# A new table of order, engines and PSUM banks for a fused attention and gated feed-forward kernel on one core

## The chip, the cores and the metric

The kernel runs on one core of a Trainium2 chip. The metric is the device time in microseconds (us) of one execution, the median of several runs. A core has five engines with a queue of instructions each: PE (TensorE, matmuls and transposes), DVE (VectorE), ACT (ScalarE), POOL (GpSimd) and SP (SyncE, which only issues transfers here).

## The reference

Eight batches, twelve heads, 448 positions, 64 elements a head. Attention's result, laid out as 448 x 768 for each batch, is the input of a gated feed-forward part with a convolution of three taps along the positions:

```python
q_n = q / sqrt(mean(q * q) + 1e-6) * g_q          # the same for k
attn = softmax(q_n @ k_n.T / 8)                   # (8, 12, 448, 448)
x = (attn @ v).transpose(0, 2, 1, 3).reshape(8, 448, 768)
h = maximum(x @ w_in, 0)                          # w_in 768 x 1024, float64
conv = sum(conv_w[k] * h shifted by k - 1 for k in range(3))   # along the 448 positions
out = (h * sigmoid(conv)) @ w_out                 # w_out 1024 x 768, float64
```

## The kernel before

Heads are worked in pairs, n = 0 to 47, six pairs to a batch. For each pair: squares of q and k (`square`), their sums and reciprocal roots (`square_sum`, `rsqrt`), q and k divided by them (`apply_rms`, 112 x 512 tiles named sq), transposes of these on PE (L812, tile sq to a bank, then copied as kT and qT), scores (L993) in groups of two tiles of 128 query rows and 448 keys, a row maximum (`soft_max`, DVE, L999, tile sst), an exponential (`soft_exp`, ACT, L1007, tile e), the transpose of e, and the product with v (pv, L1120). Pairs 0 to 9 are worked in float32: e is transposed on PE (`p_transpose`, L1038) and copied from the bank to PT (`p_evac`). From pair 10 on, operands are split into a float16 high part and a float16 low part: e into ph (`p_hi`, L438, and `p_lo`, L450), which a transfer transposes, and v into vp (`v_hi`, L442 or L444, and `v_lo`, L1105 on DVE, or two instructions on POOL). Before that a maximum of v is taken (`v_bound`, L899 or DVE's L901). A group's scores are written to two PSUM banks, and each bank is free again when the exponential of its tile has read it.

The results of six pairs make x for one batch (`x_hi`, `x_lo`). Its feed-forward part multiplies x with w_in (L1201), applies relu, the three taps and the gate, splits the result (`in_hi`, `in_lo`, tile gring), and multiplies with w_out (L1270), then copies the result out of PSUM (`out_evac`) and stores it.

w_in and w_out come as float64. Each is loaded in parts (blocks), which DVE converts to float32 by three integer instructions a part (L577, L581, L585); a bound of its absolute values is taken (L636, ACT), a power of two as scale is made from it, and each block of 128 rows is then split: `split` writes the float16 high part of a block of w_in (128 x 1024) or w_out (128 x 768), and `rest` the low part (L673 on DVE; L670 and L671, two instructions, on POOL). The trace shows these tiles as wi or wo, since they share buffers.

All of this is a list of 4,976 steps. The order is written out by hand: in the table ORDER a step has a place of two digits to the base 85, in ENGINES a letter (T PE, V DVE, A ACT, G POOL, S SP), and in BANKS the numbers of the PSUM banks that it writes. The loop at the end sorts the steps by their place and issues them, so that each engine's queue is the sorted list cut down to that engine. An engine works its queue in this order; a library puts in the waits for data and for buffers. There are 8 banks and few buffers: four e, four ph, two sq, two vp, eight v.

The lines that a choice of engine touches:

```python
def copy_scaled(e, dst, src, scale):
    if e == "ACT":
        nc.scalar.activation(dst, src, AF.Copy, scale=scale)
    else:
        elementwise(e).tensor_scalar(dst, src, scale, None, op0=ALU.mult)
...
def split(_, c):
    z = w32[:, c + 1, :]
    copy_scaled(on["split", name, c], dst[:, 0, c], z, sc)
```

Of the kernel before, what the change touches and what calls it, by code (L numbers as in the profile page):

```python
# [41 lines left out]
    bound_row="4L9X",
    bound_spread="4Q9i",
    scale="4S9l",
    in_factor="7N",
# [19 lines left out]
    rsqrt=(
        "090C0F0H0L0P0R0U0W0M0Q0S0V0X0c0f0h0k0d0m0o0s0y0&0*0<110x0z0(0+0=0_101A1E1s1u1y1#1%1;1=1^"
        "222{2|3033363D3F3I3f4t4v4x4(4-4=4@5B5F6(6+6<6?6{6}737M7R8g8k8o8s8x8$8+8=90A#A+A;A~B1BFBP"
        "BVBhDCDLDUDXDpDtDyD!D&FiFqFsF&F)F<F@F^F}H-H@H`H}I4ILITIdIhKtKuKwK&K_K~L1L7LDM;M=M?M_M|N1"
        "N2NENHP6PAPDPFPUPWPdPgPlRkRoRxR(R-R=R?R_S7T@T_T|U0U4U5U9UAUHWRWVWYWkWlWqWuW%W*Y=Y?Y_Y}Y~"
        "Z0Z2Z5Z7bNbPbSbfbhbibmbobsdXdadddmdzd%d?d_d`g8gCgFgKgLgOgQgUgYiSiViYiaibifigijipk!k#k&k*"  # L70
        "k=k@k_l7l9nZnandngnknlnnnqnvptpvpzp#p;p@p`q3q7"
    ),
# [21 lines left out]
    scores=(
        "0%0>121V1b1x1+2g2l2(373R3s3y4W4b4p525I5T5#5|6A6V6q6&787%7;8W8d8}9L9$ASAVB9BDB-B>CkCpCsDW"
        "DaE2E7EtExFHFLFOF$GtGvG_H|I2ItIxJZJdJ~K2KvKyLGLILLL?MXMZNNNQNUOCOFPTPYQ9QEQeQ!Q(RnRrR^R}"
        "S$S(S+ThTjU6USV6VBVwV#W)W=XTXmXsYNYQZ4Z8ZcZfZ_Z|a+a;bJbdbkcaccdxd$eTeXe$f1f5f&g3g6g!h6hB"
        "hHh-h?iWirjYjbkGkJlClFljl&mSmXm<m>m`nyn#o8oDo`pFpIqDqHq*q<r<r?sIsnsrtMtO"
    ),
    soft_max=(  # L100
        "0@0`16181B1K1d1q1z1)1-23262O2n2q2y2_31393K3T3m3w3z3$3)3;4c4f4r4$4}505J5L5U5X5j5n5-5?6669"
        "6N6T6j6s6%6-6@727P7U7=7?7`858f8u8#8>95979a9q9;A6AWAZAgA-BHBKBOBxB?C3C8CECrCvC&C{DEDIDbDe"
        "D(D-EAECENETE!E*E-E`FNFPFTFgFnF!F>GiGyG$G>G^G~HBI6I9IHIMI!I>I|J8JeJhJlJoK4K8KAKFK!K)K>K|"
        "LKLOLQLULjL_M4M7MaMdM*N4NRNTNXNbNkNxOJOROgOzPZPiPzP^QGQIQNQWQlQ$Q;Q^R7RDRtRwR#R&R~SHSOSU"
        "S*S;S^T0TMTQTkTnT&T?UEUOUkUoVCVHVPVTV&V_V}WBW>W^X5XDXXXeX#X(X*X~YRYTYfY$ZAZDZPZRZgZoZxZ@"
        "a6aDaUada<a^a{b0bWbZblbuc8cKcecicqc>d)d{e3eLeYecegeke;e`fBfJfNfhf=f^g7gGgkgpg)g+hGhIhRhV"
        "hYhwh{i4i6iAieiviyi{jcjgjlj?kMkXkek$lGlJlOlklyl@l{m5mZmdmumyn0n3n6nCnDnrn$n+n}oEoHoKoWoo"
        "p1pDpKpOpapcqMqPqeqlr0rBrKrMr@r`r~s4sNshsss$s_s{tPtRtXti"
    ),
# [1295 lines left out]
```

## Time and profile before

| | |
|---|---|
| median of 3 runs | 806.04 us (804.91 to 807.04) |
| time of the profiled execution | 805.12 us |
| its span in the profile | 803.3 us |
| PE busy | 780.5 us (97%) |
| DVE, ACT, POOL busy | 712.0, 637.5, 450.7 us |

The span runs from the first to the last instruction that the profiler saw, and the time of the execution is 1.82 us longer. A busy share is the part of the span in which an engine had an instruction under way. PEclk is the clock that TensorE was granted, 1.00 being 2.4 GHz and 0.50 being 1.2 GHz. Arrows in a row of the trace name the engine and tile that ended an engine's idle time.

### The profile page before, as it was taken

The page shows a single profiled execution, that of the slowest core. Times are in us where ns is not written, and L with a number is a line of the kernel's source. Part 1 is how long each engine was busy: PE and PEld are TensorE (multiplying, and loading weights), DVE is VectorE, ACT ScalarE, POOL GpSimd, SP SyncE. Part 2 cuts the span into 40 slices and gives each one's busy share as a digit, 9 for nine tenths or more (in the row PEclk, how much of TensorE's full clock was granted, in tenths as well). Part 3 has the DMA queues.
Part 4 walks back from the last instruction along what each step waited for, and adds up shares of the span by engine and source line. Part 5 has one row for each costly group of instructions (what it writes and reads, how often), then busy time and mean ns, then how long its engine had stood idle before and what let it go on. Part 6 is the DMA issues. An engine that isn't in the chain of part 4 may idle for free.

```text
span 803.3 us, 16861 instructions
## 1 busy us (share of the span) xinstructions
PE 780.5 (97%) x5564; PEld 421.6 (52%) x5564; DVE 712.0 (89%) x1489; ACT 637.5 (79%) x1542; POOL 450.7 (56%) x552
## 2 busy tenths in 40 slices
PE   3998999999999999999999999999999999999998
PEld 1545555555554555555555555555555555555554
DVE  7999999999999889998899988999999899992560
ACT  5999999997898777998788868998799767862221
POOL 2556246766478457766696646885487543530020
PEclk9999999999999999999999999999999999999999
DMA  8864653499998989999899999999999998846002
GB/s 246 236 193 116 172 179 101 97 186 208 187 199 183 195 177 209 194 182 195 188 188 199 200 181 199 207 190 197 191 189 180 209 196 182 160 91 150 12 1 79
DMA packets 345704, 137.46 MB, mean 171 GB/s; under 512 B 285376, under 2 KB 342032, under 8 KB 345616
## 3 DMA queue, kind: packets, MB, share of 16 engines
q1 hardware_dynamic: 345616, 136.37, 79.9%
q8 instruction: 44, 0.72, 0.4%
q14 instruction: 44, 0.36, 0.1%
HBM read 56.65 MB, written 11.18 MB: 84 GB/s over the span
## 4 chain that ended last, share of the span: by engine, by line
PE 55%; DVE 1%; ACT 1%; issue 1%; POOL 0%; ACTq 0%
PE bank L1270 21%; PE bank L1201 17%; PE bank L1120 7%; PE bank L993 7%; PE bank L1038 1%; PE bank L812 1%; ACT e L1007 0%; PE bank L1068 0%; DVE c L1221 0%; DVE ph L450 0%; POOL ph L450 0%; ACT PT L438 0%; ACT ph L438 0%; ACT sq L741 0%; ACT bank L1209 0%
## 5 line engine op out<-in xcount | busy, mean ns | idle before, releaser
L1201 PE MATMUL bank<-x,wi 128*128 128x448 f16 x1152 | 236.6, 353 | 0.8 <-DVE c L1231 0.6
L450 POOL TENSOR_TENSOR ph<-e,ph 128x448 f16<-128x448 f32 x139 | 148.8, 1073 | 93.9 <-ACT ph L438 60.9
L1270 PE MATMUL bank<-wo,gring 128*128 128x384 f16 (+1 forms) x1056 | 191.7, 327 | 0.0
L1201 PEld LDWEIGHTS <-wi 128*128 128x128 f16 x1152 | 110.1, 98 | 102.0 <-issue 12.8
L1270 PEld LDWEIGHTS <-gring 128*128 128x128 f16 (+1 forms) x1056 | 100.4, 99 | 65.1 <-issue 10.8
L993 PE MATMUL bank<-kT,qT 64*128 64x448 f16 (+3 forms) x1072 | 128.1, 390 | 3.8 <-ACT e L1007 2.2
L1120 PE MATMUL bank<-PT,vp 112*64 112x448 f16 x912 | 93.1, 354 | 0.0
L450 POOL TENSOR_TENSOR sq<-qkf,st 112x512 f32<-112x512 f32 x73 | 80.1, 1108 | 17.9 <-DVE st L773 7.2
L1221 DVE SCALAR_TENSOR_TENSOR c<-bank,cwb,c 128x447 f32<-128x447 f32 x128 | 85.8, 675 | 3.1 <-ACT c L442 2.1
L438 ACT CAST ph<-e 128x448 f16<-128x448 f32 x141 | 78.4, 561 | 2.1 <-DMA PT<-ph 2.0
L1120 PEld LDWEIGHTS <-vp 112*64 112x64 f16 x912 | 48.9, 110 | 41.0 <-issue 11.2
L1038 PE MATMUL bank<-ident,e 128*112 128x128 f32 x432 | 64.1, 281 | 0.0
L752 DVE TENSOR_REDUCE st<-sq 112x16 f32<-112x1024 f32 (+1 forms) x50 | 58.1, 1167 | 4.2 <-ACT sq L741 4.1
L450 DVE TENSOR_TENSOR ph<-e,ph 128x448 f16<-128x448 f32 x89 | 58.1, 655 | 2.8 <-POOL ph L450 1.2
L1038 PEld LDWEIGHTS bank<-ident,e 128*112 128x112 f32 x432 | 49.7, 136 | 20.0 <-ACT e L1007 5.6
L993 PEld LDWEIGHTS <-qT 64*128 64x128 f16 (+1 forms) x912 | 33.7, 97 | 49.4 <-issue 28.9
L442 ACT ACTIVATE c<-bank,vsc 128x384 f32<-128x384 f32 x45 | 25.8, 580 | 41.1 <-PE bank L1270 41.0
L450 POOL TENSOR_TENSOR gring<-c,gring 128x448 f16<-128x448 f32 x32 | 34.8, 1088 | 38.2 <-ACT gring L438 36.4
L741 ACT ACTIVATE sq<-qkf 112x1024 f32<-112x1024 f32 (+1 forms) x47 | 47.9, 1021 | 6.5 <-DMA qkf<-in_q_dram 4.3
L1227 ACT ACTIVATE c<-c 128x448 f32<-128x448 f32 x64 | 36.5, 573 | 17.3 <-DVE c L1221 13.7
L450 POOL TENSOR_TENSOR x<-x,x 128x448 f16<-128x448 f32 x34 | 37.9, 1116 | 21.7 <-DVE x L438 15.2
L450 POOL TENSOR_TENSOR qkf<-sq,qkf 112x512 f16<-112x512 f32 x35 | 42.5, 1213 | 9.9 <-DVE qkf L438 6.1
(1148 smaller groups left out, 1588.0 us busy)
## 6 DMA issues: line engine op xcount, KB each, us to landing
qkf<-in_k_dram SPq DMA_DIRECT2D x48, 224.0 KB
v<-in_v_dram SPq DMA_DIRECT2D x48, 224.0 KB
rB<-rd SPq DMA_DIRECT2D x96, 112.0 KB
out_dram<-c SPq DMA_DIRECT2D x56, 192.0 KB
wo<-in_moe_w_in_dram SPq DMA_DIRECT2D x12, 512.0 KB
gring<-in_moe_w_out_dram SPq DMA_DIRECT2D x16, 384.0 KB
qkf<-in_q_dram SPq DMA_DIRECT2D x24, 224.0 KB
qkf<-in_q_dram SPq DMA_DIRECT2D x48, 112.0 KB
```

The costliest lines, as they stand in the source:

```text
L438: (nc.scalar.copy if e == "ACT" else elementwise(e).tensor_copy)(dst, src)
L442: nc.scalar.activation(dst, src, AF.Copy, scale=scale)
L450: elementwise(e).tensor_tensor(dst, a, b, op=op)
L741: nc.scalar.activation(sq, x, AF.Square)
L752: nc.vector.tensor_reduce(st, sq, axis=AX.X, op=ALU.add)
L993: nc.tensor.matmul(ps[u][o, :S], lhs, rhs, start=(i == 0), stop=(whole(m) or i == 2),)
L1038: nc.tensor.transpose(ps[:PB, kt * P : (kt + 1) * P], e[:, kt * PB : (kt + 1) * PB], ident)
L1120: nc.tensor.matmul(ps[HALF[h], :S], lhs, rhs, start=(i == 0 and k == 0), stop=(i == pvs(n)[-1] and k == NB - 1),)
L1201: nc.tensor.matmul(ps[:, :S], wi[:, wl, c, fc * P : (fc + 1) * P], old("x", b * NP + c)[:, xl], start=(i == 0), stop=(i == 3 * NP - 1),)
L1221: nc.vector.scalar_tensor_tensor(c[:, dst], h[:, src], w[:, tap, fc : fc + 1], c[:, dst], op0=ALU.mult, op1=ALU.add)
L1227: nc.scalar.activation(c, c, AF.Tanh)
L1270: nc.tensor.matmul(ps[p0 : p0 + m, :NO2], g, wo[:, wl, fc, half * NO2 : (half + 1) * NO2], start=(i == 0), stop=(i == 3 * NFC - 1),)
```

## The change

The code stays as it is; the numbers in ORDER, ENGINES and BANKS are others. Of the table ORDER two lines show the form:

```diff
-    split="4Z4o4*4~5p5(9p9y9<A5AKAsA<B8",
+    split="4Y4q4+4|5l6M9p9z9=A2ALAzA~BM",
```

The letters that give a step to another engine, for four of the names:

```diff
-    split="A",
+    split="AAAAAGAAAAAAAG",
-    square="AAAAAAGAAGAAAGAAAAAAAAAAAAAAAAAAAAAAAAAAAAAAAAAAAA",
+    square="AAAAAAGAAGGAAGAAAAAAAAAAAAAAAAAAAAAAAAAAAAAAAAAAAA",
-    v_hi="AAAAAAVAAAAAAAAAVVVAAAAAAAAAAAAAAAVAAV",
-    v_lo="V",
+    v_hi="AAGGAAAAAAVGGVAAAAAGGVAAAAAGAAVAAAGGAV",
+    v_lo="VVVVVVVVVVVVVVVVVVVVVGVVVVVVVVVVVGGGGV",
```

So POOL (G) gets the split of block 5 of w_in and of the last block of w_out, the square of pair 8, nine of the 38 `v_hi` and five of the 38 `v_lo`. Counted over all names, before and after: `p_evac` 103 on ACT and 5 on DVE, then 97 and 11; `p_hi` 45 on POOL, 141 on ACT and 42 on DVE, then 60, 134 and 34; `p_lo` 139 on POOL and 89 on DVE, then 137 and 91; `x_lo` 34 on POOL and 14 on DVE, then 38 and 10; `in_hi` 18 on POOL, 38 on ACT and 8 on DVE, then 16, 35 and 13; `in_lo` 38 on POOL and 26 on DVE, then 35 and 29; `out_evac` 45 on ACT and 11 on DVE, then 40 and 16. `convert` stays on DVE and the bounds of the weights on ACT. PE has the same steps in both, and so has SP, in slightly other orders.

Three places are shown in the order of one engine.

PE, where pair 4's scores begin; e0 and e1 are tiles of pair 3 that are transposed, sq_5 is pair 5's normalized q and k, kT_4 and qT_4 the operands of pair 4's scores. A group of scores writes two banks. Before:

```order
L1038 MATMUL bank2_68<-ident_83,e0_74 112x128 x4
L1038 MATMUL bank3_69<-ident_83,e1_75 112x128 x4
L558 LDWEIGHTS ones_85
L558 MATMUL bank7_73<-mrow_84,ones_85 128x1
L812 MATMUL bank6_72<-ident_83,sq_5_513 128x112 x4
L993 MATMUL bank4_70<-kT_4_686,qT_4_710 128x448
L993 MATMUL bank1_67<-kT_4_686,qT_4_710 128x448
L993 MATMUL bank2_68<-kT_4_686,qT_4_710 128x448
L993 MATMUL bank5_71<-kT_4_686,qT_4_710 128x448
L993 MATMUL bank4_70<-kT_4_686,qT_4_710 128x448
L993 MATMUL bank3_69<-kT_4_686,qT_4_710 128x448
```

The same place now:

```order
L812 MATMUL bank3_69<-ident_83,sq_5_510 128x112 x4
L558 LDWEIGHTS ones_85
L558 MATMUL bank7_73<-mrow_84,ones_85 128x1
L993 MATMUL bank1_67<-kT_4_703,qT_4_676 128x448
L993 MATMUL bank4_70<-kT_4_703,qT_4_676 128x448
L1038 MATMUL bank7_73<-ident_83,e0_74 112x128 x4
L1038 MATMUL bank6_72<-ident_83,e1_75 112x128 x4
L993 MATMUL bank2_68<-kT_4_703,qT_4_676 128x448
L993 MATMUL bank5_71<-kT_4_703,qT_4_676 128x448
L993 MATMUL bank4_70<-kT_4_703,qT_4_676 128x448
L993 MATMUL bank3_69<-kT_4_703,qT_4_676 128x448
```

Two transposes of pair 3 now stand between the first group of scores and the second, and the third group's first bank, bank 4, is held by the first group's second tile and no longer by its first.

ACT, the same place; PT_3 is a copy of a transposed tile of pair 3, e0 and e1 from sst_(4_0 and sst_(4_1 are the exponentials of pair 4's first two tiles, wi32 with wsc a split of w_in. Before:

```order
L1007 ACTIVATE e3_77,rsum_3_611<-bank4_70,sst_(3_6_667 128x448
L438 COPY PT_3_642<-bank2_68 112x4x128
L442 ACTIVATE wi32_92<-wi32_92,wsc_96 128x1024
L442 ACTIVATE kT_5_764<-bank6_72,G_82 128x448
L438 CAST x_1_770<-x32_1_671 128x448
L438 COPY PT_3_642<-bank3_69 112x4x128
L1007 ACTIVATE e0_74,rsum_4_776<-bank4_70,sst_(4_0_761 128x448
L442 ACTIVATE wi32_92<-wi32_92,wsc_96 128x1024
L1007 ACTIVATE e1_75,rsum_4_776<-bank1_67,sst_(4_1_766 128x448
```

And now:

```order
L1007 ACTIVATE e3_77,rsum_3_597<-bank4_70,sst_(3_6_668 128x448
L442 ACTIVATE kT_5_738<-bank3_69,G_82 128x448
L438 COPY PT_3_640<-bank2_68 112x4x128
L442 ACTIVATE wi32_92<-wi32_92,wsc_96 128x1024
L438 COPY PT_3_640<-bank5_71 112x4x128
L1007 ACTIVATE e0_74,rsum_4_771<-bank1_67,sst_(4_0_762 128x448
L1007 ACTIVATE e1_75,rsum_4_771<-bank4_70,sst_(4_1_765 128x448
L438 COPY PT_3_640<-bank7_73 112x4x128
L442 ACTIVATE wi32_92<-wi32_92,wsc_96 128x1024
L438 COPY PT_3_640<-bank6_72 112x4x128
```

The two exponentials now follow each other, the cast of x_1 has left ACT, and two copies of PT stand behind the exponentials.

POOL, about pairs 6 to 8; sq_6 and sq_7 with st are `apply_rms`, x_3 and x_4 high and low parts of x, rsum the denominators. Before:

```order
L450 TENSOR_TENSOR sq_6_722<-qkf_6_525,st_6_721 112x2x4x64
L438 CAST x_3_980<-x32_3_963 128x448
L1062 TENSOR_SCALAR rsum_5_892<-rsum_5_892 128x7
L450 TENSOR_TENSOR sq_7_753<-qkf_7_665,st_6_721 112x2x4x64
L450 TENSOR_TENSOR x_3_980<-x32_3_963,x_3_980 128x448
L438 CAST x_4_1105<-x32_4_1093 128x448
```

And now, where the row with 112x1024 is the square of pair 8 and the row with 128x1024 the split of block 5:

```order
L450 TENSOR_TENSOR sq_6_723<-qkf_6_636,st_6_722 112x2x4x64
L450 TENSOR_TENSOR sq_8_985<-qkf_8_709 112x1024
L450 TENSOR_TENSOR sq_7_746<-qkf_7_670,st_6_722 112x2x4x64
L438 CAST x_3_1016<-x32_3_979 128x448
L450 TENSOR_TENSOR x_3_1016<-x32_3_979,x_3_1016 128x448
L444 TENSOR_SCALAR wi32_92<-wi32_92,wsc_96 128x1024
L1062 TENSOR_SCALAR rsum_5_891<-rsum_5_891 128x7
L438 CAST x_4_1114<-x32_4_1095 128x448
```

Both new rows stood on ACT before.

## Rows read from the trace of the kernel before

**Rows 1.** The page's busy time, share of the span and instructions of each engine

```profile
PE 780.5 (97%) x5564; PEld 421.6 (52%) x5564; DVE 712.0 (89%) x1489; ACT 637.5 (79%) x1542; POOL 450.7 (56%) x552
```

**Rows 2.** Windows: stretch, length, busy PE, PEld, DVE, ACT, POOL, PEclk, DMA share, GB/s

```profile
0.00:10.60 10.60, 0.01 (x1) 0.01 (x1) 6.02 (x28) 3.99 (x7) 2.79 (x11) 1.00 0.71 212
10.60:62.38 51.78, 46.75 (x271) 25.51 (x271) 50.77 (x128) 47.83 (x124) 24.15 (x34) 1.00 0.80 219
62.38:66.00 3.62, 1.77 (x8) 0.69 (x9) 3.52 (x5) 3.62 (x8) 2.98 (x2) 1.00 0.81 260
66.00:71.00 5.00, 5.00 (x26) 3.93 (x26) 4.98 (x10) 4.51 (x9) 3.80 (x9) 0.66 0.47 113
71.00:101.61 30.61, 30.29 (x192) 15.78 (x191) 30.23 (x61) 30.22 (x75) 11.83 (x18) 1.00 0.55 149
101.61:780.00 678.39, 676.97 (x4931) 365.19 (x4930) 615.24 (x1261) 543.84 (x1317) 403.39 (x478) 1.00 0.84 171
780.00:803.30 23.30, 19.68 (x143) 10.54 (x140) 1.24 (x2) 3.49 (x6) 1.72 (x2) 1.00 0.19 68
```

**Rows 3.** PE's waits, whole span: bank and line, releaser, us, times, longest

```profile
PE bank L812 <- POOL sq L450: 11.1, 2, 10.6
PE bank L993 <- ACT e L1007: 2.2, 2, 1.8
```

**Rows 4.** PE's longest wait between 101 and 780 us, same columns

```profile
PE bank L1201 <- DVE c L1231: 0.6, 1, 0.6
```

**Rows 5.** PE in time: start, length, instruction, [idle before, releaser]

```profile
62.38 1.77 PE L993 MATMUL bank<-kT,qT 64*128 64x448 f32 x8
66.00 1.02 PE L993 MATMUL bank<-kT,qT 64*128 64x448 f32 x4 [1.84 <-ACT e L1007]
66.95 4.08 PE L1038 MATMUL bank<-ident,e 128*112 128x128 f32 x20
...
85.03 0.60 PE L812 MATMUL bank<-ident,sq 112*128 112x112 f32 x4
...
98.77 1.96 PE L1038 MATMUL bank<-ident,e 128*112 128x128 f32 x16
...
101.61 1.31 PE L1201 MATMUL bank<-x,wi 128*128 128x448 f16 x6
```

**Rows 6.** One window of 1 us, columns as in rows 2

```profile
67.00:68.00 1.00, 1.00 (x7) 0.99 (x6) 1.00 (x3) 0.60 (x2) 0.60 (x2) 0.50 1.05 222
```

**Rows 7.** ACT in time: the exponential of pair 4's first tile

```profile
65.19 0.67 ACT L1007 ACTIVATE e<-bank,sst_(4_0_761 128x448 f32<-128x448 f32 x1
```

**Rows 8.** ACT's groups: shapes, count, busy us, mean ns, idle before

```profile
L438 ACT COPY PT<-bank 112x512 f32<-112x512 f32 x68 | 38.3, 598 | 0.9 <-PE bank L1038 0.5
L438 ACT CAST x<-x 128x448 f16<-128x448 f32 x24 | 13.5, 563 | 1.9 <-DVE x L1131 1.9
L899 ACT ACTIVATE vabs<-v 112x512 bf16<-112x512 f32 x29 | 18.3, 631 | 1.0 <-DVE vacc L896 0.7
L442 ACT ACTIVATE wi<-wi,wsc 128x1024 f16<-128x1024 f32 x6 | 7.1, 1182 | 0.0
L741 ACT ACTIVATE sq<-qkf 112x1024 f32<-112x1024 f32 x43 | 45.4, 1058 | 0.7 <-issue 0.7
```

**Rows 9.** Groups of POOL, and one of DVE, same columns

```profile
L670 POOL TENSOR_SCALAR wo<-wo,wsc 128x768 f32<-128x768 f32 x1 | 2.2, 2212 | 0.0
L438 POOL CAST qkf<-sq 112x512 f16<-112x512 f32 x10 | 6.7, 672 | 0.3
L450 POOL TENSOR_TENSOR ph<-e,ph 128x448 f16<-128x448 f32 x139 | 148.8, 1073 | 93.9 <-ACT ph L438 60.9 <-DVE ph L438 18.0 <-issue 3.4
L450 DVE TENSOR_TENSOR ph<-e,ph 128x448 f16<-128x448 f32 x89 | 58.1, 655 | 2.8 <-POOL ph L450 1.2 <-ACT ph L438 0.9 <-issue 0.4
```

**Rows 10.** POOL and DVE in time: a square on POOL, the rest of block 5

```profile
62.50 1.89 POOL L450 TENSOR_TENSOR sq<-qkf 112x1024 f32<-112x1024 f32 x1 [7.48 <-PE bank L812]
...
92.39 1.28 DVE L673 SCALAR_TENSOR_TENSOR wi<-wi,wsc 128x1024 f16<-128x1024 f32 x1
```

More of the change, by code (lines that the diff above doesn't have):

```diff
@@ L30 @@
     load_g="05",
-    make_g="0Y",
-    load_cw="3=6e4j",
+    make_g="0X",
+    load_cw="3H6S5|",
     make_cw="8(",
-    load="02080K0N0u0;0|1e1k2I2j2-2>3O4T4Y5D5Q5)626a6p7G7O7(868Z8v",
+    load="02080J0N0g0;1H1X1h1?2j2+2<3h4S4d5B5W5;5^6j6r7G7Y7-868b8y",
     convert=(
-        "0A0D0G0g0i0t0!0)0-0}131S1P1Z1f1v1$1}1?2V2f2a2i2)2c2$42353a452}3P3^3h3r3|4C4F4O4A4D4I4<53"
-        "5851555E5r5x5$5v5_5}6L6Q6W6f6i6l6|767B797E7J7p7w7!7*7}828K8O8T8j8l8q8`91999B9D9J"
-    ),
-    bound="0J0$0?2~2M2B2@2^4E4B44497q6X6d7T7L7k7<8h7)7n8a8e98969F9O",
@@ L40 @@
-    bound_max="4H9R",
+        "0A0D0G0h0j0v0$0*0<111A1T1R1W1e1v1$1+212V2d2R2i2(2m2$43393W3|2{3O413f3p3@4C4F4N4A4D4I4;52"
+        "57545A5J5r5z5&5w5$5+6W6d6h6f6i6o75787C7E7K7N7r7y7&7=7~828N8P8W8k8p8t8_8}949B9D9G"
+    ),
+    bound="0q0%0@2^202F312;4E4B48457D6e5}7s7d6)7(8D7?7b8l8U969C989L",
+    bound_max="4H9Q",
     bound_turn="4J9U",
[L42 to L45, printed above, removed]
-    split="4Z4o4*4~5p5(9p9y9<A5AKAsA<B8",
-    rest="4i4w4^5a5y6Y9u9&9`ABARA$B2Bq",
@@ L48 @@
-    out_factor="A!",
+    bound_row="4L9Y",
+    bound_spread="4O9d",
+    scale="4R9g",
+    in_factor="7H",
+    split="4Y4q4+4|5l6M9p9z9=A2ALAzA~BM",
+    rest="4j4x4@5Z5t6Y9u9*9`AAAUA+B5Bv",
+    out_factor="A%",
     load_k=(
-        "00040T0q1M2F2<3-4a5s6J7j7~9+AzCMDRElFuG-IKJXKnMCNIOGPvQ#R@T4UmVjWWY5Z$anbrcoe!fSgwh!j>j~"
-        "mRmwo|p3"
+        "00040S0s1k2L3u3=465p6J7l8B9$AsCNDPE(G6G%ILJaKpM6M(OJPiQ;ScTKU{VRWhY2ZaaicPckd{fNgqhzjVj~"
+        "lkmzo<o`"
     ),
     load_q=(
-        "030B0a0#1t2R3j464d5+6=7m8^9>A&CQD_EyG6G`I#JjK*MGN`OUP@Q&SgTIU?VlX8YBZ(aqcScre%fVg|h&j_k3"
-        "mqm!p0p7"
+        "030B0b0w1p2P3y3}4g626P7u8)9)AwCRD=E@GSG-J4JeLYM9NrONPnQ?SnTWVIVfWnY7ZjaocVcoeefRgzh%j=k3"
+        "mhm&o@o}"
@@ L64 @@
+        "ktkzn9nOpYph"
     ),
     rsqrt=(
[L66 to L70, printed above, removed]
@@ L93 @@
+        "oKoZoboc"
     ),
     scores=(
[L95 to L98, printed above, removed]
+        "0&0>131U1c1y1(2g2l2&383S3s3x4Q4k4p505H5X5<5`666Z6$6*797$7;8c8f8|9K9-ASAYB8BDB-B>CoCrCwDN"
@@ L103 @@
[L103 to L107, printed above, removed]
@@ new lines @@
+        "s`t*uZug"
+    ),
+    v_max="2O7hDSL|RCaBg!oi",
+    v_turn="2T7pDuMASQaHg)ol",
+    v_row="2a7vEKMCSqaJg>oo",
+    v_spread="2f7!ETMISuaXh4or",
+    v_scale="2r7*EWMKSwabh8ox",
+    qk_lo="9oAxClDDE`F7GwH;K1KvL*MNO6O*Q&RaTXUHVCWFXfYyZ)atcJdue#fog}hrjEkKmZm;oAo>q&rp",
+    q_hi="9V9XByCiD}FCGJGyIvJ_LJL+NlNjP;QlSfT3UoVKXBYSZnaGbzccesflh9h3j0j$l^m*oSoHqYrQ",
+    q_lo="9a9kB*CnE3FFGOG+I!J~LsM3NsOWP@Q^SkTHUtVvXKYaZ$ajb)cneyf$hDh?j6j|l|n2oYokqdrV",
+    q_turn="9lAZB_CxEOFNGYH&I;KBL!MTN!O!QARTSrT$U#V}XcYoa6b0b^d6e*f<hLiDjjk_mQn7ogpaqqsF",
@@ L266 @@
+        "tcuRuxu8wVwQwHwawFwSwgwj"
     ),
```

336 lines of the change are left out of this document (168 added, 168 removed).

## The prediction

> **What bounds the kernel now.** The page's busy times come first: PE is busy for 780.5 of 803.3 us [rows 1], so whatever the table does elsewhere can only reach the time through PE, and PE has the same 5,564 matmuls before and after. Three things of PE can move: its idle time, its clock, and what it loses between instructions of different kinds. The windows say where these lie [rows 2]; in each the reader should compare the length with PE's busy time. The span has 22.8 us without a matmul: 10.6 at the start, 5.0 up to 62.38, 1.85 from there to 66, 0.3 from 71 to 101.61, 1.4 in the 678 us up to 780, and 3.6 at the end. The list of PE's waits names them: one wait of 10.6 us for the first normalized tile, and one of 1.8 us in which scores wait for an exponential [rows 3]. After 101 us the longest is 0.6 us [rows 4].
>
> The wait of 1.84 us is the one to look at closely. In PE's timeline [rows 5] two groups of pair 4's scores run at 62.38, and the third starts at 66.00, released by ACT. Directly behind it the granted clock falls: it is 0.50, the 1.2 GHz level, in the window from 67 to 68 [rows 6] and 0.66 on average from 66 to 71, against 1.00 in every other stretch [rows 2]. Twenty transposes then take 4.08 us where sixteen take 1.96 at the full clock [rows 5]. The fall costs 5.0 x 0.34 = 1.7 us; the transposes alone give 4.08 - 1.96 x 20 / 16 = 1.6, which agrees. So this place costs 3.5 us, a third of the 10 us that PE loses between its start and its tail.
>
> Last come the other engines' shares in the same windows. From 62.38 to 101.61 ACT is busy for 38.4 of 39.2 us and DVE for 38.7; from 101.61 on ACT has 135 us to spare, DVE 63 and POOL 275 [rows 2]. So until about 101 us PE's progress is set by ACT and DVE, whose exponentials free the score banks; later it is set by PE itself.
>
> **The start.** Up to the first scores the rows of DVE, POOL and SP are the same in the order of both, and ACT and DVE have the same steps ahead of the exponentials of pairs 0 and 1. Nothing is taken for it, neither gain nor loss.
>
> **The wait at 66 us.** Before, the third group's first bank is held by pair 4's first tile, whose exponential starts at 65.19 and takes 0.67 [rows 7], so it ends just when PE starts. Now the bank is held by the second tile. Ahead of that exponential ACT loses two copies of PT and the cast of x_1: 2 x 0.598 + 0.563 = 1.76 us by the means of their groups. It gains the second exponential, 0.67 by the first's row, and the bound of v for pair 6, 0.63 [rows 7, 8]. Net, the release comes 0.46 earlier; instructions on ACT overlap by about 0.1 us, so I take **0.3 us**. From both sides: nothing, if the two copies were hidden behind other waits, and 1.0 if the bound is hidden.
>
> What becomes of the idle time is less plain. The two transposes of pair 3 that ran ahead of the scores now stand between the first and second group, and the second group's banks come free by copies that stand behind a split on ACT (1.18 us [rows 8]). So the one wait is cut into two or three, some of it ahead of the first group, with 1.1 us of transposes and 0.9 of scores in between. I expect no single stretch as long as 1.84 us, and the only such stretch in the trace that is followed by a lower clock after the start is that one. My forecast is that the fall goes: **-1.7 us**, with 0 as the other end, if a stretch of that length merely moves forward.
>
> **What the lead can be worth.** -0.3 and -1.7 would be -2.0 at 71 us, but it has to survive to 101.61, through a stretch in which ACT is full. Ahead of the last exponentials there ACT loses two casts of x (0.56 each), the split of block 5 (1.18), the square of pair 8 (1.06) and a copy of PT (0.60), together 3.96; it gains a bound of v (0.63), a copy of PT (0.60), and two short steps that I bound by 0.6 each, together 2.4 [rows 8]. The difference, -1.5, is how much sooner ACT can be through. ACT's idle time from 66 to 101.61, 0.49 + 0.39 [rows 2], could be squeezed out as well, which makes 2.4 the upper end. DVE gives up three of the steps that ACT gains and one more, some 1.8 us or more at ACT's prices, so ACT is the limit. I take the lesser of 2.0 and 1.5: **-1.5 us** in all up to 101.61, between 0 and -2.4.
>
> **POOL's new work before 101 us.** The square of pair 8 took 1.06 on ACT [rows 8], and a square of this size took 1.89 on POOL [rows 10]. The split of 128 x 1024 has no row on POOL. The nearest are a scaling of 128 x 768 in 2.21 us, by length 2.95, and a cast of 112 x 512 in 0.67, by length 1.34 [rows 9]. The first is the same operation, so I take 2.95 and keep 1.34 as the other end. From 71 to 101.61 POOL is idle for 18.8 us [rows 2], which hides both as long as their results are not asked for first; the case where they are is the rival below. The Trainium skill (GPSIMD Engine Reference, section 4.1, Engine selection) says that elementwise operations with two inputs are about twice as slow on GpSimd as on VectorE, and with one input roughly as fast. The trace shows 1073 against 655 ns, 1.6 times, for two inputs [rows 9], and it disagrees for one: by that rule the split would take little over 1 us, and 2.21 us for 768 columns does not fit it. By the rule the sum stays as it is and the rival loses its ground; by the row the rival stands.
>
> **From 101 us on.** POOL takes nine high parts of v, 0.67 to 1.47 us each (the same two rows, the second by length), five low parts, two instructions each of together up to 1.47 + 1.07, and fifteen high parts of e at about 0.67: up to 36 us [rows 9], with 275 idle. Cover is shortest for pair 45, where both parts of v stand on POOL and seven steps of PE lie between the first and the product that reads them. A step of PE is 780.5 / 1,246 = 0.63 us, so the cover is 4.4 us against 1.47 + 2.54 = 4.0 of work; with one or two low parts of e late ahead of it (1.07 each) PE would wait 0.7 to 1.8. I take **+0.3**; the lower end is -1.4, all that PE waits there now. PE changes from one kind of step to another 604 times, where it was 596. Rows 5 show the next kind starting 0.07 us before the modelled end of the last (66.00 + 1.02 against 66.95), so I take 0 and let 8 x 0.1 = 0.8 stand for the range.
>
> **The tail.** The 3.6 us behind the last matmuls are a copy out of PSUM and a store. Both stay, so 0.
>
> **The sum.** The profiled execution took 805.12 us, 0.92 below the median of 806.04. -1.5 + 0.3 = -1.2 gives 803.9 for such an execution, and **804.8** as a median. A measurement of this kernel can tell about 0.3%, or 2.4 us, from no change, so this counts as the same.
>
> **Rivals.**
>
> *The wait only moves.* PE reaches the first group of pair 4 sooner, since two transposes were taken from ahead of it, and then stands for a copy or an exponential as long as before, and the clock falls all the same. For it: ACT is full from 62.38 to 66 [rows 2], and its load ahead of this place falls by only 0.46. Then nothing is gained but what later stretches bring: **806.0**.
>
> *A larger lead.* The fall goes, and ACT's idle time with it: -2.4, and nothing is lost from 101 on, or some of the 1.4 there is won (-0.3). Own time 802.4, median **803.3**.
>
> *The split on POOL comes late (the other side).* POOL's square of pair 8 needs the buffer of pair 6's tile, whose last transposes run on PE at 85.03 for 0.60 [rows 5]; a square on POOL that had to wait for such a buffer stands in rows 10, with 7.48 us. From 85.6: 1.89 for the square, 1.1 for pair 7's tile, 0.6 and 1.1 for x_3, then 2.95 for the split makes 93.2. DVE's low part of the block, which reads the split, ran at 92.39 [rows 10], and with 1.8 us less ahead of it on DVE would come at about 90.6. DVE then stands for 2.5 us with a row maximum queued behind, PE runs out of scores for most of that, and the clock falls again: +2.5 + 1.7 - 1.5 = +2.7 on 806.04, **808.7**. It decides when the split ends more than about 1 us after DVE asks; with 1.34 for the split it ends at 91.6, and nothing happens. On the same page of the Trainium skill, section 8 (Key points) says that GpSimd shares its SBUF interfaces with VectorE; no row here isolates that, and it would only lengthen the split.
>
> **How the numbers follow.** Chances: the forecast 44%, the wait that only moves 24%, the larger lead 17%, the late split 15%. The forecast's own range is 803.7 to 805.8. The range runs from 802.9, which leaves out half of the larger lead's low side, to 808.0, which leaves out the worse half of the late split. Faster by over 0.3% (under 803.6): the larger lead and a little of the forecast, 0.19. Slower (over 808.4): the late split where it is worst and an unforeseen wait, 0.14. The rest, 0.67, is no change that can be told.
>
> **What would show it.** Right: PEclk 1.00 in all windows from 60 to 75 us; no wait of PE over 1.5 us after its start; the first product with w_in (101.61 before [rows 5]) at about 100.1; PE's idle time from there to 780 at 1 to 2 us. Wrong: a window at 0.50 anywhere from 58 to 100 us; DVE waiting for POOL at the low part of block 5; waits of PE for vp behind POOL after 700 us.

## The result, and the profile after

The changed kernel took 813.09 us as a median (811.34 to 813.65), the kernel before 805.47 in the same comparison; the ratio is 1.0089, with a 95% interval of 1.0066 to 1.0112. It is slower by 7.6 us by the medians and by 7.2 by the ratio (5.3 to 9.0 by its interval), where 804.8 and no change that can be told were forecast.

The profiled execution has a span of 811.1 us, 7.8 more than before. The page's busy times after, to be held against [rows 1]:

```profile
PE 781.6 (96%) x5564; PEld 423.0 (52%) x5564; DVE 728.3 (90%) x1510; ACT 615.7 (76%) x1497; POOL 499.2 (62%) x584
```

PE is busy for 1.1 us more with the same matmuls; idle time went from 22.8 to 29.5. ACT has 22 us less to do, DVE 16 and POOL 49 more. The windows tell where the idle time came in; columns as in [rows 2]:

```profile
62.38:66.00 3.62, 3.62 (x14) 2.39 (x14) 3.62 (x5) 3.62 (x9) 3.54 (x3) 0.53 0.88 231
66.00:71.00 5.00, 4.76 (x32) 2.65 (x30) 5.00 (x10) 4.80 (x9) 3.79 (x9) 1.00 0.39 110
...
101.61:780.00 678.39, 670.59 (x4866) 361.98 (x4865) 625.34 (x1271) 522.26 (x1268) 447.18 (x508) 1.00 0.85 171
```

The idle time came in where PE hardly waited before: from 101.61 to 780 us PE is idle for 7.8 us, where it was 1.4. Ahead of it little has changed. The clock fell once more, only sooner (0.53 from 62.38 to 66, against 0.66 from 66 to 71 [rows 2]), and the first product with w_in starts at 101.45, 0.16 earlier than in [rows 5]. From that product to the end of the span it is 709.7 us, against 701.7 before: 8.0 us, the whole loss.

PE's timeline from 101 us on names the waits; the first row is the first product with w_in, the others are six of the eleven waits over 0.3 us, among them the four longest:

```profile
101.45 1.31 PE L1201 MATMUL bank<-x,wi 128*128 128x448 f16 x6
...
204.57 0.27 PE L1068 MATMUL bank<-ident,rsum 128*7 128x128 f32 x1 [0.50 <-ACT e L1007]
...
220.47 0.28 PE L1068 MATMUL bank<-ident,rsum 128*7 128x128 f32 x1 [0.64 <-ACT e L1007]
...
362.10 0.28 PE L1068 MATMUL bank<-ident,rsum 128*7 128x128 f32 x1 [2.23 <-ACT e L1007]
...
496.28 0.76 PE L993 MATMUL bank<-kT,qT 64*64 64x448 f16 x12 [0.33 <-ACT e L1007]
497.42 0.74 PE L993 MATMUL bank<-kT,qT 64*128 64x448 f16 x6 [0.38 <-ACT e L1007]
...
716.04 0.74 PE L993 MATMUL bank<-kT,qT 64*128 64x448 f16 x6 [1.22 <-ACT e L1007]
```

All six wait for an exponential, and ACT has time to spare there. So the next question is what ACT waited for. At the longest, the rows of POOL, ACT and DVE are these:

```profile
353.93 1.57 POOL L444 TENSOR_SCALAR vp<-v,vsc 112x512 f16<-112x512 f32 x1
355.45 2.99 POOL L438 CAST gring<-c 128x448 f16<-128x448 f32 x1
358.39 0.56 POOL L438 CAST ph<-e 128x448 f16<-128x448 f32 x1
359.03 2.02 POOL L450 TENSOR_TENSOR ph<-e,ph 128x448 f16<-128x448 f32 x2
...
360.10 0.63 ACT L1007 ACTIVATE e<-bank,sst_(23_4_4576 128x448 f32<-128x448 f32 x1 [3.28 <-POOL ph L450]
...
355.44 0.68 DVE L450 TENSOR_TENSOR qkf<-sq,qkf 112x512 f16<-112x512 f32 x1
356.04 0.62 DVE L450 TENSOR_TENSOR gring<-c,gring 128x448 f16<-128x448 f32 x1
356.57 0.62 DVE L450 TENSOR_TENSOR ph<-e,ph 128x448 f16<-128x448 f32 x1
357.11 0.38 DVE L438 CAST ph<-e 128x448 f16<-128x448 f32 x1
357.41 0.62 DVE L450 TENSOR_TENSOR gring<-c,gring 128x448 f16<-128x448 f32 x1
```

The exponential of pair 23's fifth tile has its row maximum at 355.51 and its bank, but none of the four tiles e: one comes free only when a low part of e has been taken from it, and the low parts of pair 23 stand on POOL behind the high part of v of pair 22 (1.57 us) and a cast that took 2.99 us. ACT stands for 3.28 us, PE for 2.23. At 496 and 716 us ACT stood for low parts of e as well (0.99, 0.96 and 0.80 us). At 204 and 220 us it did not: there it stood 2.62 and 2.45 us for DVE. At 204 us:

```profile
202.00 0.63 ACT L1007 ACTIVATE e<-bank,sst_(13_3_2429 128x448 f32<-128x448 f32 x1 [2.62 <-DVE sst_(13_3_2429 L999]
...
200.31 1.03 POOL L450 TENSOR_TENSOR ph<-e,ph 128x448 f16<-128x448 f32 x1 [0.33 <-DVE vsc L1184]
...
200.32 1.05 DVE L1185 TENSOR_SCALAR cwb<-cw,vsc 128x24 f32<-128x24 f32 x1
```

The DVE instruction, ahead of the row maximum, is one of eight of its kind with a median of 0.24 us; here it takes 1.05, as long as POOL's beside it. Such pairs come up again below.

Behind the wait at 362 us the clock falls:

```profile
362.00:367.00 5.00, 4.87 (x20) 2.35 (x21) 5.00 (x8) 3.72 (x10) 4.02 (x5) 0.66 0.88 175
```

That is 5.0 x 0.34 = 1.7 us more. PE's new idle time after the first product, 6.4, and this 1.7 make 8.1, the 8.0 that were lost. The clock's part is not in every execution: the four have mean granted clocks of 0.995 to 1.000, and the one at 1.000 took 811.34 us, 6.5 more than the 804.8 that the kernel before takes at 1.000 on average (37 executions).

### The profile page after: what moved, and what is told of

Read it like the earlier page. It is cut to its first block, busy times and chain, and to the rows that moved or that the text cites. A ratio compares the mean times of both kernels' runs of the same rounds, so it can differ in the third digit from the quotient of the medians.

```text
span 811.1 us, 16921 instructions
## 1 busy us (share of the span) xinstructions
PE 781.6 (96%) x5564; PEld 423.0 (52%) x5564; DVE 728.3 (90%) x1510; ACT 615.7 (76%) x1497; POOL 499.2 (62%) x584
## 4 chain that ended last, share of the span: by engine, by line
PE 67%; DVE 15%; ACT 7%; POOL 6%; issue 4%; DMA 1%; SPq 0%; DVEq 0%; POOLq 0%; ACTq 0%
PE bank L1270 24%; PE bank L1201 19%; PE bank L1120 9%; PE bank L993 9%; PE bank L1038 3%; ACT e L1007 2%; PE bank L812 2%; DVE c L1221 2%; POOL ph L450 1%; DVE st L752 1%; DVE ph L450 1%; ACT PT L438 1%; POOL sq L450 1%; DVE c L1231 1%; DVE wo L673 1%
## 5 line engine op out<-in xcount | busy, mean ns | idle before, releaser
L993 PE MATMUL bank<-kT,qT 64*128 64x448 f16 (+3 forms) x1072 | 127.8, 390 | 4.4 <-ACT e L1007 1.9
L450 POOL TENSOR_TENSOR sq<-qkf,st 112x512 f32<-112x512 f32 x71 | 77.9, 1109 | 24.0 <-DVE st L773 7.1
L438 ACT CAST ph<-e 128x448 f16<-128x448 f32 x134 | 74.3, 562 | 2.2 <-issue 1.3
L450 DVE TENSOR_TENSOR ph<-e,ph 128x448 f16<-128x448 f32 x91 | 60.4, 665 | 7.3 <-ACT ph L438 4.8
L993 PEld LDWEIGHTS <-qT 64*128 64x128 f16 (+1 forms) x912 | 34.2, 97 | 52.2 <-issue 31.9
L442 ACT ACTIVATE c<-bank,vsc 128x384 f32<-128x384 f32 x40 | 23.0, 577 | 36.7 <-PE bank L1270 35.0
L450 POOL TENSOR_TENSOR x<-x,x 128x448 f16<-128x448 f32 x38 | 42.3, 1112 | 11.6 <-DVE x L438 5.1
```

What stands on the lines that cost most here:

```text
L438: (nc.scalar.copy if e == "ACT" else elementwise(e).tensor_copy)(dst, src)
L450: elementwise(e).tensor_tensor(dst, a, b, op=op)
L993: nc.tensor.matmul(ps[u][o, :S], lhs, rhs, start=(i == 0), stop=(whole(m) or i == 2),)
```

## Experiments

Theory 1 came from those rows: parts of v on POOL hold up the low parts of e behind them. Theory 2 is that the loss is spread over the new table. The changes are to ENGINES unless ORDER or BANKS is named; G is POOL, A ACT, V DVE. In the first four kernels the tables take fewer lines, so L993 reads L781 there, and so on by 212.

**v off POOL in the changed kernel** (e1_v_off_pool).

```diff
-    v_hi="AAGGAAAAAAVGGVAAAAAGGVAAAAAGAAVAAAGGAV",
-    v_lo="VVVVVVVVVVVVVVVVVVVVVGVVVVVVVVVVVGGGGV",
+    v_hi="AAAAAAAAAAVAAVAAAAAAAVAAAAAAAAVAAAAAAV",
+    v_lo="VVVVVVVVVVVVVVVVVVVVVVVVVVVVVVVVVVVVVV",
```

> The changed kernel with one thing undone: the nine high parts of v on POOL go to ACT and the five low parts on POOL to DVE, at the places in the order that they have. Theory 1 (parts of v on POOL, 1.57 to 2.9 us each, hold up the low parts of e behind them in POOL's queue, tiles e come free late, and scores wait): the waits of PE at 362 us (2.2 us, and the fall of the clock behind it, 1.7), 496 (0.7), 716 (1.2) and 211 us (0.3) go, 813.1 - 6.1 = 807.0 us, 806 to 809. Theory 2 (the loss is spread over the whole new table, with VectorE at 90% and more, and v has no special part in it): 811 to 813 us, with waits of the same sum at other places.

808.54 us (807.44 to 810.36), 1.0046 of before (1.0032 to 1.0060): of the loss, 4.6 of 7.6 us are gone by the medians, 3.5 of 7.2 by the ratios. The waits at 204, 211, 220 and 362 us and the fall of the clock are not in the profile; 0.38 us are left at 496 and 0.16 at 716, and waits of 0.62 and 0.58 are new at 312 and 708. So parts of v on POOL are about half of the loss or somewhat more. About 3 us stay, in waits of 0.6 us at most, of which theory 1 says nothing.

**v on POOL in the kernel before** (e2_v_on_pool).

```diff
-    v_hi="AAAAAAVAAAAAAAAAVVVAAAAAAAAAAAAAAAVAAV",
-    v_lo="V",
+    v_hi="AAGGAAVAAAAGGAAAVVVGGAAAAAAGAAAAAAGGAV",
+    v_lo="VVVVVVVVVVVVVVVVVVVVVGVVVVVVVVVVVGGGGV",
```

> The kernel before with one thing of the change: the same nine high and five low parts of v on POOL, in the old order. Theory 1: slower than before by 3 to 6 us, 808.5 to 811.5 us, with new waits of PE for exponentials that follow a part of v on POOL within 10 us. Theory 2: POOL's idle time hides them, 805 to 806.5 us.

813.77 us (811.64 to 815.85), 1.0107 (1.0090 to 1.0124): the same fourteen parts cost 8.5 us in the old order, more than expected. PE's waits, columns as in [rows 3]:

```profile
PE bank L781 <- DVE x L919: 3.2, 2, 2.9
...
PE bank L781 <- ACT rT L226: 2.1, 1, 2.1
```

The 2.1 us end at 710.73, 2 us after two low parts of 2.7 us each left POOL, and ACT stood for 2.25 us for a low part of e on POOL there, as theory 1 has it. The 2.9 us end at 347.87, 5 us after the high part of pair 22 left POOL, but not by that way, since ACT and PE both wait for DVE. The rows of POOL, ACT and DVE, and last DVE's row at the same place in the kernel before:

```profile
341.46 1.57 POOL L232 TENSOR_SCALAR vp<-v,vsc 112x512 f16<-112x512 f32 x1
343.00 1.03 POOL L238 TENSOR_TENSOR ph<-e,ph 128x448 f16<-128x448 f32 x1
...
346.20 0.58 ACT L1015 ACTIVATE c<-c 128x448 f32<-128x448 f32 x1 [2.84 <-DVE c L1009]
...
341.22 4.35 DVE L238 TENSOR_TENSOR sq<-qkf,st 112x512 f32<-112x512 f32 x2
...
340.08 1.41 DVE L450 TENSOR_TENSOR sq<-qkf,st 112x512 f32<-112x512 f32 x2
```

Two instructions of DVE with two inputs take 4.35 us instead of 1.41, while POOL runs the part of v and what is behind it without a pause. So here the part of v cost by a second way: instructions of DVE beside POOL's became longer. The last two experiments have such pairs alone. Behind each of the two waits the mean clock is 0.66 over 5 us.

**All new letters in the old order, and the other way round** (e3_new_letters, e4_new_order). In the first, every letter in the kernel before is the new one; in the second, every letter in the changed kernel is the old one. One line stands for all:

```diff
-    split="A",
+    split="AAAAAGAAAAAAAG",
...
-    split="AAAAAGAAAAAAAG",
+    split="A",
```

> The old order and banks with all the new engine letters. Theory 1: at least as slow as the run with v alone on POOL in the old order, 809 to 814 us. Theory 2, where the order is what costs: 805 to 808 us; where the letters cost as a whole and not v: more than 3 us slower than the run with v alone.

> The new order and banks with all the old engine letters (v on ACT and DVE). Theory 1: like the changed kernel without v on POOL, 806 to 809 us. Theory 2, where the order is what costs: 811 to 814 us.

888.0 us (1.1019, interval 1.1004 to 1.1034) and 861.99 us (1.0703, interval 1.0682 to 1.0724). Both expectations missed by far. Order and letters are fitted to each other: either half of the new table in the other's company costs 57 to 83 us, so no share of the 7.6 us can be given to the order or to the letters as wholes. Single letters, as in the other runs, can be tried.

**One part of v at another place on POOL** (e5_v22_later), a change to ORDER: the high part of pair 22 (Qy) goes to the place R8, behind three low parts of e (two of them on POOL), and the 33 steps in between move up by one.

```diff
-    v_hi="BnDrErF8F;IyJ%KaMRMgM?ORQyRfT8TLUZW_XrZ3aeayb~ctfBgDhChXkAkNmHmeo#pMpNs4s~tO",
+    v_hi="BnDrErF8F;IyJ%KaMRMgM?ORR8RfT8TLUZW_XrZ3aeayb~ctfBgDhChXkAkNmHmeo#pMpNs4s~tO",
```

> The changed kernel with one step at another place: the high part of v of pair 22, on POOL (1.57 us), comes behind the three low parts of e of pair 23 that it stood ahead of, so POOL has the same work. Theory 1 (place in POOL's queue decides): the low parts come 1.6 us earlier, PE's wait at 362 us shrinks from 2.2 to about 0.7 us, the clock does not fall there, 813.1 - 3.3 = 809.8 us, 809 to 811. Rival (POOL's amount of work, or VectorE, decides): 812.5 to 813.5 us, the wait stays over 1.5 us.

815.3 us (813.84 to 816.71), 1.0125 (1.0109 to 1.0142): 2 us worse, not 3 better. The wait for the exponential is gone as expected, and a longer one has come:

```profile
363.09 2.51 DVE L1105 SCALAR_TENSOR_TENSOR vp<-v,vsc,vp 112x512 f16<-112x512 f32 x1 [1.58 <-POOL vp L444]
...
366.19 4.13 PE L1270 MATMUL bank<-wo,gring 128*128 128x384 f16 x14 [3.25 <-DVE gring L450]
```

Now DVE stands for 1.58 us for the high part, since it takes the low part from it, and then needs 2.51 us for what takes 0.85 on average before, while POOL runs two low parts of 1.03 us each from 363.03 on; a low part of gring queues behind it, and PE waits for that. So it is not only what is behind the part on POOL: early, the part holds up POOL's queue, late, it holds up DVE's.

**That part on ACT** (e6_v22), **and the long cast on ACT** (e7_inhi26), each alone in the changed kernel.

```diff
-    v_hi="AAGGAAAAAAVGGVAAAAAGGVAAAAAGAAVAAAGGAV",
+    v_hi="AAGGAAAAAAVGAVAAAAAGGVAAAAAGAAVAAAGGAV",
...
-    in_hi="GGGGAAAAVGGAGGAAAAAVAAGAAAGGAAAVAGGGAAAVAAVAAAAAVAAAVVVVAVVAGGVA",
+    in_hi="GGGGAAAAVGGAGGAAAAAVAAAAAAGGAAAVAGGGAAAVAAVAAAAAVAAAVVVVAVVAGGVA",
```

> The changed kernel with the high part of v of pair 22 alone on ACT, all other parts of v as changed. Theory 1: as if it came later on POOL, 809 to 811 us, and the other three places (211, 496, 716 us) wait as before. Rival: 812.5 to 813.5 us.

> The changed kernel with one cast of gring on ACT, the one that took 2.99 us on POOL at 355.45 while VectorE ran five instructions with both inputs in SBUF back to back. Theory 1 with that stretch as part of the cause: the low parts behind it come up to 3 us earlier, the wait at 362 us and the fall of the clock go, 813.1 - 3.9 = 809.2 us, 808.5 to 810.5. Rival (the cast only filled time in which POOL would have waited for VectorE or ACT anyway): over 811.5 us, the wait stays.

The first gives 810.36 us (809.18 to 811.08), 1.0064 of before (1.0052 to 1.0076): 2.7 less than the changed kernel by the medians, 2.0 by the ratios, with no wait and no fall of the clock near 362 us, the waits at 496 and 716 us as before, and one of 0.90 new at 315. One instruction of 1.57 us on an engine that is 62% busy cost 2.0 to 2.7 us. The second gives 812.11 us (810.97 to 813.32), 1.0081 (1.0068 to 1.0094): 1.0 less, which is not clear of noise. The wait shrinks to 0.67 us and the clock stays at 1.00 behind it, but 0.54 and 0.55 us are new at 412 and 421. The long cast was a part of that wait; what it costs in all these runs cannot tell.

**Parts of v at single places in the old order** (e14_v_12_13, e15_v_43_46).

```diff
-    v_hi="AAAAAAVAAAAAAAAAVVVAAAAAAAAAAAAAAAVAAV",
+    v_hi="AAGGAAVAAAAAAAAAVVVAAAAAAAAAAAAAAAVAAV",
...
-    v_hi="AAAAAAVAAAAAAAAAVVVAAAAAAAAAAAAAAAVAAV",
-    v_lo="V",
+    v_hi="AAAAAAVAAAAAAAAAVVVAAAAAAAAAAAAAAAGGAV",
+    v_lo="VVVVVVVVVVVVVVVVVVVVVVVVVVVVVVVVVGGGGV",
```

> The kernel before with the high parts of v of pairs 12 and 13 alone on POOL. If it is POOL's amount of work that costs (the run with all fourteen parts in the old order lost 8.5 us): 2/9 of the high parts, about 1 us, 806 to 806.5 us. If the place decides: nothing, 804.8 to 805.6 us, no new wait of PE between 180 and 240 us.

> The kernel before with two high parts (pairs 44, 45) and four low parts (43 to 46) of v alone on POOL. If the place decides: PE waits 2.1 us at about 703 us and the clock falls behind it, as in the run with all fourteen, 808 to 809.5 us. If the loss needs all fourteen parts: 805 to 806 us.

The first took 805.15 us (ratio 1.0000, 0.9992 to 1.0009): two parts at a place with slack cost nothing. The second took 808.85 (1.0046, 1.0033 to 1.0060): six parts cost 4 us where slack is short. The second also gives POOL more work, some 14 us against 3, so the times alone do not part the place from the amount. Its rows show the mechanism of theory 1 in the old order:

```profile
695.49 1.04 POOL L450 TENSOR_TENSOR ph<-e,ph 128x448 f16<-128x448 f32 x1 [0.17 <-ACT ph L438]
696.50 1.58 POOL L1102 TENSOR_SCALAR v<-v,vsc 112x512 f32<-112x512 f32 x1
698.16 1.17 POOL L1103 TENSOR_TENSOR vp<-v,vp 112x512 f16<-112x512 f32 x1
699.29 1.15 POOL L450 TENSOR_TENSOR qkf<-sq,qkf 112x512 f16<-112x512 f32 x1
700.43 1.56 POOL L1102 TENSOR_SCALAR v<-v,vsc 112x512 f32<-112x512 f32 x1
702.07 1.16 POOL L1103 TENSOR_TENSOR vp<-v,vp 112x512 f16<-112x512 f32 x1
703.18 1.03 POOL L450 TENSOR_TENSOR ph<-e,ph 128x448 f16<-128x448 f32 x1
...
704.25 0.63 ACT L1007 ACTIVATE e<-bank,sst_(46_2_9414 128x448 f32<-128x448 f32 x1 [2.25 <-POOL ph L450]
...
705.16 0.74 PE L993 MATMUL bank<-kT,qT 64*128 64x448 f16 x6 [2.11 <-ACT rT L438]
```

Two low parts of v of 2.7 us each and a low part of q or k stand between two low parts of e, 6.7 us in all; ACT waits 2.25 us for the tile, and PE, whose bank is freed by the next copy on ACT, 2.11. The clock is 1.00 in the windows around it, so that part of the expectation failed.

**What is left of the loss** (e8_dve_lighter, e10_weights_back, e11_p_hi_act): each has v off POOL as the first run, and one edit more. Only e10's letters are short enough to stand whole; in e8 every V of `out_evac`, `in_hi` and `in_relu` becomes A, in e11 every G of `p_hi`.

```diff
-    split="AAAAAGAAAAAAAG",
-    square="AAAAAAGAAGGAAGAAAAAAAAAAAAAAAAAAAAAAAAAAAAAAAAAAAA",
+    split="AAAAAAAAAAAAAA",
+    square="AAAAAAGAAGAAAGAAAAAAAAAAAAAAAAAAAAAAAAAAAAAAAAAAAA",
```

> The changed kernel with v off POOL, and besides 37 steps of VectorE given to ACT at the places that they have: 16 copies of the result, 13 high parts of gring, 8 relus. Theory 3 (what is left of the loss, about 3 us, comes from VectorE, which has 15 us more work than before, so row maxima come late): 805 to 807 us. Rival (order and letters are fitted to each other, so any such move costs): 808.5 us or more, with waits for ACT.

> The changed kernel with v off POOL, and the split of block 5, the split of the last block of w_out and the square of pair 8 back on ACT too, at the places that they have. Theory 4 (these hold POOL up as v does, before 101 us and at the wait of 0.4 us at 163): 807.5 us or less, against 808.5 with v alone. Rival (their places are slack for POOL, and ACT is full up to 101 us): 808.5 us or more, and the stretch from the first scores to the first product with w_in grows from 87.0 us.

> The changed kernel with v off POOL, and all 60 high parts of e on POOL given to ACT, at the places that they have. Theory 4 (POOL's load is what is left of the loss, about 3 us): 805 to 807 us, the waits of 0.4 to 0.6 us at 312, 492 and 708 us go. Rival (order and letters are fitted to each other; ACT is late where it gets them): over 809 us.

808.72 us (808.45 to 809.55), 808.37 (806.96 to 810.42) and 815.48 (815.22 to 816.2), where v alone gave 808.54. DVE's load is not it: with 37 steps fewer it is busy for 712.3 us, as much as in [rows 1], and nothing is won. POOL's share of the weights is not it either, as far as these runs can tell. Moving all high parts of e off POOL costs 7 us. The 3 us stay open: waits of 0.15 to 0.6 us at some ten places. At the three longest with v alone, at 312, 337 and 708 us, the way leads to DVE: PE waits for it at 337, and ACT had stood for it, 2.82 and 1.19 us, at the other two. That POOL holds up single instructions of DVE there is a rival that no run takes apart.

**The wait and the clock at 66 us, in the kernel before** (e12_banks_4_6): banks 4 and 6 exchanged in BANKS from the third group of pair 4's scores on. One line:

```diff
-    sum_transpose="571036443031253573745105345117222402222434321541",
+    sum_transpose="571034663031253573745105365117222602222636321561",
```

> The kernel before with banks 4 and 6 exchanged from the third group of pair 4's scores on, so that this group no longer waits for the first tile's exponential, but for a copy of PT that ends 0.67 us sooner; work, order and engines are as before. By the prediction's step on the clock (the wait of 1.84 us becomes 1.2, the clock stays at 1.00, and ACT's idle time lets the lead through): 0.7 + 1.7 sooner at 71 us, up to 0.9 at 101 us, 804 to 804.5 us. By what the runs so far show (ACT is the limit up to 101 us): the first product with w_in moves by 0 to 1 us, 804.5 to 805.5 us, the same as before.

805.28 us, ratio 0.9999 (0.9990 to 1.0008). The wait of 1.84 us is now one of 0.27 and one of 0.68, and the clock falls all the same. PE in time:

```profile
65.50 1.96 PE L993 MATMUL bank<-kT,qT 64*128 64x448 f32 x4 [0.27 <-ACT kT L442]
67.38 0.65 PE L1038 MATMUL bank<-ident,e 128*112 128x128 f32 x4
68.72 3.49 PE L1038 MATMUL bank<-ident,e 128*112 128x128 f32 x16 [0.68 <-ACT e L1007]
```

The window behind it, columns as in [rows 2]:

```profile
66.00:71.00 5.00, 4.32 (x19) 2.99 (x18) 5.00 (x9) 4.91 (x11) 4.23 (x7) 0.75 0.77 187
```

So a fall does not need one long wait, and taking that wait apart is worth nothing. Nor does the long wait bring the fall each time. The kernel of e14, which is the kernel before up to here, has the same wait in its profile, and the clock stays at 1.00 (PE in time, and the window behind it):

```profile
66.12 1.02 PE L993 MATMUL bank<-kT,qT 64*128 64x448 f32 x4 [1.84 <-ACT e L1007]
67.08 2.85 PE L1038 MATMUL bank<-ident,e 128*112 128x128 f32 x20
...
66.00:71.00 5.00, 4.83 (x30) 2.87 (x32) 5.00 (x10) 4.96 (x12) 3.92 (x9) 1.00 0.52 128
```

From the start of the third group to the first product with w_in, at 100.82, it is 34.70 us here and 35.61 with the fall [rows 5]: the fall costs 0.9.

**POOL beside VectorE** (e9_two_engines, e13_two_engines): a kernel that computes nothing of the reference, whose core is pairs such as

```python
for i in range(16):
    nc.gpsimd.tensor_copy(ph[:, s], pe[:, s])
    nc.vector.tensor_tensor(dl[:, s], de[:, s], dh[:, s], op=ALU.subtract)
```

> A kernel that computes nothing of the reference: 16 instructions at a time on POOL, on VectorE (DVE) or on both, in eight stages that wait for each other, output zeros. Theory of exclusion (an instruction of VectorE with both inputs in SBUF and an instruction of POOL keep each other out): the cast of 128x448 takes 0.56 us alone and beside an instruction of VectorE with one input or one in PSUM, and 1.0 to 1.2 us beside one with two inputs in SBUF; the scaled copy of 112x512, 1.57 alone, takes 2.1 beside it. Rival (the long ones in the traces had another cause, such as transfers): all within 10% of alone.

> The stages of the kernel that computes nothing of the reference once more, now strictly one after the other on both engines (in the first form VectorE's instructions of several stages ran mixed). Theory of exclusion: the cast of 128x448 on POOL takes 0.56 us alone, beside an instruction of VectorE with one input in PSUM (L77) or one input (L82), and about 1.0 us beside one with two inputs in SBUF (L72); the scaled copy of 112x512 is 1.57 alone and longer beside L91, and the two-input instructions L95 and L96 stretch each other. Rival: no pair differs from alone by more than 10%.

In the first form VectorE's instructions of several stages ran mixed, so its means tell little (the cast alone 620 ns on average, with VectorE's others in between 692 to 853). In the second form, groups of one stage each, columns as in [rows 8]:

```profile
L63 POOL CAST ph<-pe 128x448 f16<-128x448 f32 x16 | 8.9, 557 | 0.9
L71 POOL CAST ph<-pe 128x448 f16<-128x448 f32 x16 | 13.0, 815 | 0.9
L76 POOL CAST ph<-pe 128x448 f16<-128x448 f32 x16 | 8.9, 557 | 0.9
L81 POOL CAST ph<-pe 128x448 f16<-128x448 f32 x16 | 8.9, 557 | 0.9
L86 POOL TENSOR_SCALAR ph<-pe,sc 112x512 f16<-112x512 f32 x16 | 25.0, 1563 | 1.5
L90 POOL TENSOR_SCALAR ph<-pe,sc 112x512 f16<-112x512 f32 x16 | 25.6, 1600 | 1.5
L95 POOL TENSOR_TENSOR pl<-pe,ph 128x448 f16<-128x448 f32 x16 | 20.4, 1278 | 1.2
...
L67 DVE TENSOR_TENSOR dl<-de,dh 128x448 f16<-128x448 f32 x16 | 10.0, 624 | 0.5
L72 DVE TENSOR_TENSOR dl<-de,dh 128x448 f16<-128x448 f32 x16 | 13.6, 852 | 0.5
L96 DVE TENSOR_TENSOR dl<-de,dh 128x448 f16<-128x448 f32 x16 | 20.8, 1302 | 0.5
```

L63 is the cast alone; beside it VectorE has two inputs in SBUF in L71, one of two in PSUM in L76, one input (a row maximum) in L81. Only the first stretches it, by 46%, and VectorE by 37% (624 to 852 ns, L67 and L72); where both engines have two inputs, VectorE's takes 1302 ns (L96). The scaled copy takes 1563 ns alone (L86), nearly three times the cast, and 1600 beside two inputs in SBUF (L90), so it is hardly stretched, against the expectation. The theory of exclusion is right in kind for the cast and for two inputs; the cast's size is below the 1.0 us expected, and the 2.99 us, the 2.51 and the 4.35 for two in the kernels are beyond what this shows. In those three the other engine worked without a pause: DVE ran five instructions, four of them with two inputs, from 355.44 to 358.03 beside the cast of 2.99 us. That this is the reason is not shown.

## Why the prediction was wrong

**The failed step is "From 101 us on", the term of +0.3.** It measured +8.0 in the profiled executions. The prediction set up to 36 us of new work on POOL against 275 us of POOL's idle time, and looked for the shortest cover only between a part of v and the product that reads it. It did not ask what is queued behind the part on POOL. That is the low parts of e, which give the four tiles e back, and so the next exponential, the scores' bank and PE. Nor did it ask what POOL's instructions do to DVE's beside them: it had the sharing of interfaces down as something that could only lengthen the split, and the longest wait of e2 came through longer instructions of DVE. Parts of v on POOL cost 3.5 to 4.6 us in the new order (e1) and 8.5 in the old (e2), by both ways together; one part alone is worth 2.0 to 2.7 (e6). POOL's idle time, 40% from 101 us on, was no cover: at some places its work is asked for within a microsecond or two, at others not (the rows at 362 us and of e15, against e14). The rest of the +8.0 stays open.

**Pair 45**, the place singled out, was priced at 0.7 to 1.8 us; the trace shows 1.22 at 716 us, by way of the tiles e and not of the product that reads v. The other places, pairs 12, 22 and 31, were not looked for.

**The prices of the parts** were nearly right: a median of 1.57 us for a high part, where 0.67 to 1.47 was the range, 2.7 to 3.3 for a low part, where 2.54 was the sum, and 2.85 for the split of block 5, where 2.95 was taken. The rule of the Trainium skill that the prediction named (GPSIMD Engine Reference, section 4.1, Engine selection) has one-input work on GpSimd at roughly line rate. For the cast of e the trace before is near it, with means of 602 ns on POOL and 436 on DVE; for the high part of v the trace after is far from it, with 1627 and 519.

**The lead of -1.5 us up to 101 us** measured -0.16. The rival "the wait only moves" is right in that the clock fell all the same, ahead of pair 4's second group, and nothing was gained; but no wait for a copy or an exponential came ahead of it, only 0.97 and 0.35 us for DVE ahead of the first group. The worth of the fall was mis-sized as well. In 52 executions of the kernel before, 37 have a mean granted clock of 1.000 and take 804.8 us on average, and 15 have 0.998, as the profiled one has, and take 805.8. So a fall of this size is in three of ten executions and goes with 1.0 us, not 1.7, as the 0.9 from e14's trace has it too. The median has no fall that could be taken away; the median of three that the sum starts from, 806.04, is also 1.0 above the 805.1 of these 52. The new order reaches the first product with w_in at 101.45 us with the fall and at 101.83 without (e1), the old order at 101.61 and at 100.82 (e14). So in two profiles without the fall the new order is later there by 1.0 us, or 0.75 counted from the first scores, and not earlier.

**The late split** came as a wait of DVE of 1.26 us for POOL at 91.47, half of the 2.5 in the rival, and PE waited 0.98 us at 95.25 without a fall of the clock. Putting the split back on ACT (e10) changed nothing in the time that can be told.

**The forecast of "slower"** had a chance of 0.14, nearly all by a place ahead of 101 us that turned out harmless. The rival on the other side was the wrong mechanism.

What stays open is about 3 us of the loss, how the rest divides between the tiles e and DVE's longer instructions, the 2.99 us of one cast, and what decides whether the clock falls.

## What to carry to other kernels

Before a step goes to an engine that is idle much of the time, look at what stands behind it in that engine's queue and how soon it is asked for; the share of idle time says nothing of that, and one instruction of 1.6 us ahead of a step that returns a scarce buffer cost 2.0 to 2.7 us here. Look also at what the other engine runs beside it: work given to POOL made instructions of DVE longer. A table of order and a table of engines that were fitted together are one thing: either half without the other was 57 to 83 us slower. And read a loss such as a lower clock in more than one execution before putting it in the sum: the profiled one may be the exception.
